# Turning token tiles on VectorE in 32x32 blocks, with x gathered from DRAM in quarter rows

## The chip, the cores and the metric

The kernel runs on one core of a Trainium2 chip. The metric is the device time of one execution in microseconds (us); several executions are summed up by their median. The profile shows one profiled execution of the same program: its span, from the first to the last instruction, is a little shorter than that execution's time, which also holds what lies around it.

## The reference

Two blocks follow each other. The first is a linear attention with decay; its result, the heads laid side by side, is x, with 512 features for each of 4 x 768 = 3,072 tokens. The second is a mixture of 8 experts in which a token can keep the expert of the token before it:

```python
def _moe_ref(x, w_gate, w_local, w1, w2):
    ...
    for b in range(B):
        prev_e = -1
        for s in range(S):
            fresh_e = int(np.argmax(logits[b, s]))
            if s == 0 or local_gate[b, s] < 0.5:
                e = fresh_e
            else:
                e = prev_e if prev_e >= 0 else fresh_e
            prev_e = e
            ...
            h = np.maximum(x[b, s] @ w1[e], 0.0)
            out[b, s] = p[e] * (h @ w2[e])
```

Each token goes through one expert only: 512 features to 1,024 hidden ones, and back to 512. Everything is float32.

## The kernel before, in words

**Attention, 24 steps.** A step takes 128 tokens of one sequence (6 chunks x 4 sequences). It loads 1 MB of q, k and v into one of six buffers `inp` (`loaded`, L156, from the SP queue, five steps ahead), multiplies by decays on GpSimd (`prepare`), and makes scores, the part from the state, and the mix with v on TensorE (`scores`, `from_state`, `mix`). The result `xc` lies with features in the partitions. One step later `rows_of` (L241) turns it with four TensorE transposes into token rows, copies them on ScalarE from PSUM into `xn`, and stores them from ScalarE's DMA queue as 128 rows of `x_dram`, 2 KB each. `xn` has two buffers.

**Routing, between the steps.** After each four steps `gates` and `logits` make the gate logits. The table `extras` (L665) hangs the routing work on fixed steps: which expert each token has, which rank among that expert's tokens, and, inverted, which token sits in each of the 128 slots of an expert tile. `by_slots` (L547) makes this inversion with small matmuls against one-hot masks; from its result it computes `gidx`, the row of `x_dram` for each slot, and `rows_out` (L573) computes `sidx`, the row of the output. This is done twice: for the first five tiles (KA = 5), which only need the tokens of the first 12 steps, during the attention; and for all others while the first expert tiles run (from `brought(1, ...)` on, L768). `span(i)` gives the tiles of each of the two sets.

**Experts.** In this data there are 24 full tiles of 128 slots and 3 half tiles of 64 tokens. For each full tile g:

- `ahead(g)` (L625) calls `collect` (L619): one indirect DMA from GpSimd fetches the 128 rows of the tile into `xgt[g % 2]`, slot by slot in the partitions;
- `turned(g)` (L633) makes four 128x128 transposes on TensorE into a PSUM tile `po1`, and VectorE copies the result to `xtt[g % 2]`, features in the partitions (L637). For tile 0 `first_turned` (L628) does the same in the PSUM tile `pr`;
- `hidden(g, half)` (L639) multiplies by w1: 64 matmul records of 128 columns (each float32 matmul shows as two), ReLU on ScalarE;
- `output(g)` (L650) multiplies by w2 into PSUM: 16 records of 512 columns;
- `written(g)` (L655): VectorE scales by the token's probability into `y`, and GpSimd scatters the rows to the output with an indirect DMA.

`weights(g)` (L608) loads the 2 MB of w1 and the 2 MB of w2 of a tile's expert from the SP queue, when the expert differs from that of the tile two before. Half tiles run beside full ones (`ahead_half`, `turned_half`, `hidden_of_half`, `output_of_half`, L784 to L831). They carry 64 tokens, every one in two partitions, and are turned in four transposes as well.

**What sets the order.** TensorE, VectorE and SP execute in the order in which the program is written (`manual_schedule`); ScalarE's and GpSimd's orders come from a scheduler. [...] In the expert loop, `turned(g + 1)` stands between `hidden(g, 1)` and `output(g)`, and `ahead(g + 2)` ahead of `hidden(g, 0)`. The order at the start of the experts is: the last `mix`, `rows_of(22)`, `first_turned`, `hidden(0, 0)`, `rows_of(23)`, `gates(5)`, `ahead(2)`, `hidden(0, 1)`. Completion of GpSimd's DMAs is signalled on eight semaphores, which the DMAs take in turn; an issue waits until the last one on the same semaphore has landed.

Of the kernel before, what the change touches and what calls it, by code (L numbers as in the profile page):

```python
# [8 lines left out]
F32 = mybir.dt.float32  # L9
# [33 lines left out]
CA = 3  # L43
NA = B * CA
PARTS = [(0, 8), (8, NA), (NA, NT)]
LOADS = 6
QUARTERS = [5, 9, 13, 17]
WARM = 10
# [12 lines left out]
def kernel(  # L61
# [13 lines left out]

    dram = ctx.enter_context(tc.tile_pool(name="dram", bufs=1, space=bass.MemoryType.DRAM))
    x_dram = dram.tile([N, DM], F32, name="x_dram")
    lt = route.tile([P, NT, E + 1], F32, name="lt")  # L80
    moe = ctx.enter_context(tc.tile_pool(name="moe", bufs=2))
    rt = ctx.enter_context(tc.tile_pool(name="rt", bufs=1))
# [158 lines left out]
    def rows_of(s):  # L241
        px = pg.tile([P, DM], F32, name="pk1")
        for a in range(A):
            nc.tensor.transpose(px[:, P * a:P * a + P], xc[:, a, ORDER[s][0]], ident)  # L244
        xn = moe.tile([P, DM], F32, name="xn")
        nc.scalar.copy(xn, px)  # L246
        nc.scalar.dma_start(out=x_dram[P * s:P * s + P, :], in_=xn)

    def gates(k):

# [23 lines left out]
    beforeb = const.tile([P, P], BF16, name="beforeb")  # L274
    dupb = const.tile([P, P], BF16, name="dupb")
    upper = const.tile([P, 1], F32, name="upper")
    ones8 = const.tile([P, E], F32, name="ones8")
    down = const.tile([P, E], F32, name="down")
    go = [const.tile([P, E, hi - lo + 1], BF16, name=f"go{i}") for i, (lo, hi) in enumerate(PARTS)]
# [16 lines left out]
    def constants_2():  # L296
        nc.vector.tensor_copy(count, ints[0][:, :G + 1])
        nc.vector.tensor_copy(whole, ints[0][:, P:P + G + 1])
        nc.vector.tensor_copy(identb, ident)
        nc.vector.tensor_scalar(down, count[:, :E], -1.0, float(E), ALU.mult, ALU.add)  # L300

    def constants_3():
# [6 lines left out]
    def constants_4():  # L309
        for half in range(2):  # L310
            nc.vector.tensor_copy(dupb[:, HP * half:HP * half + HP], ident[:, :HP])
        nc.vector.tensor_reduce(upper, ident[:, HP:], axis=AX.X, op=ALU.add)


    gidx = [route.tile([P, n], U32, name=f"gidx{i}") for i, n in enumerate((KA, G - KA))]
    sidx = [route.tile([P, n], U32, name=f"sidx{i}") for i, n in enumerate((KA, G - KA))]
    gate = [route.tile([P, n], F32, name=f"gate{i}") for i, n in enumerate((KA, G - KA))]
    owner = [route.tile([1, n], I32, name=f"owner{i}") for i, n in enumerate((KA, G - KA))]
# [97 lines left out]
    def chances(i):  # L416

        lo, hi = PARTS[i]
        n = hi - lo
        if i == 2:  # L420
            room = act.tile([P, DM], F32, name="room", bufs=1)
        else:
            room = att.tile([P, DM], F32, name="kd", bufs=3)
        prob = room[:, :n * E].rearrange("p (n e) -> p n e", e=E)
        den, pick = (room[:, k:k + n] for k in (n * E, n * (E + 1)))
        nc.vector.tensor_tensor(prob, lt[:, lo:hi, :E], nows["mx", i].unsqueeze(2).broadcast_to([P, n, E]), ALU.subtract)
        nc.scalar.activation(prob, prob, ACT.Exp)
        nc.vector.tensor_reduce(den, prob, axis=AX.X, op=ALU.add)
        nc.vector.tensor_scalar(den, den, 1e-9, None, ALU.add)
        nc.vector.reciprocal(den, den)  # L430
        nc.vector.tensor_tensor(prob, prob, hot_of(i).rearrange("p e t -> p t e"), ALU.mult)
        nc.vector.tensor_reduce(pick, prob, axis=AX.X, op=ALU.add)
        nc.vector.tensor_tensor(pick, pick, den, ALU.mult)
        for k in range(2, 5):
            nc.vector.tensor_copy(parts[:, lo:hi, k], pick)
            if k < 4:
                nc.vector.tensor_tensor(pick, pick, parts[:, lo:hi, k], ALU.subtract)

    def span(i):
        return ((0, KA), (KA, G))[i]  # L440
# [106 lines left out]
    def by_slots(i, ks):  # L547

        (g0, g1), val = span(i), nows["val"]
        w = g1 - g0  # L550
        pinv = pr[:, 2 * P:2 * P + len(ks) * w]
        cols = [(j, t) for j in range(2 + i) for t in range(PARTS[j][1] - PARTS[j][0])]
        for j, t in cols:
            nc.tensor.matmul(pinv, lhsT=onehots[j][:, t],
                             rhs=val[:, PARTS[j][0] + t].rearrange("p k g -> p (k g)"),
                             start=(j, t) == cols[0], stop=(j, t) == cols[-1], skip_group_check=True)
        got = pools[i].tile([P, len(ks), w], F32, name=f"got{i}_{ks[0]}", bufs=1)
        nc.vector.tensor_copy(got, pinv.rearrange("p (k g) -> p k g", k=len(ks)))
        if 0 in ks:

            src = nows["src"] = pools[i].tile([P, w], F32, name=f"src{i}", bufs=1)
            nc.vector.tensor_scalar(src, got[:, 0], -float(P), 0.0, ALU.add, ALU.max)
            nc.vector.tensor_tensor(gidx[i], src, got[:, 1], ALU.add)
            nows["got"] = got
        if i:
            few = nows["few"] = act.tile([P, len(ks), E], BF16, name="few", bufs=1)
            nc.vector.tensor_copy(few, got[:, :, w - E:])
        if 4 in ks:
            k = ks.index(2)
            nc.vector.tensor_tensor(got[:, k], got[:, k], got[:, k + 1], ALU.add)  # L570
            nc.vector.tensor_tensor(gate[i], got[:, k], got[:, k + 2], ALU.add)

    def rows_out(i):  # L573

        got = nows["got"]
        nc.vector.tensor_scalar(got[:, 0], got[:, 0], 0.0, float(SKIP), ALU.is_equal, ALU.mult)
        nc.vector.tensor_tensor(sidx[i], got[:, 0], gidx[i], ALU.add)

    def both_halves():

# [31 lines left out]
        nc.sync.dma_start(out=w2t[g % 2], in_=w2_src(e), cond=other, cond_hint=False)  # L612


    xgt = [moe.tile([P, DM], F32, name=f"xg{i}", bufs=1) for i in range(2)]
    xtt = [moe.tile([P, DT, P], F32, name=f"xt{i}", bufs=1) for i in range(2)]
    pys = []

    def collect(xg, i, j):  # L619
        n = N if i else NA * P  # L620
        nc.gpsimd.indirect_dma_start(out=xg, out_offset=None, in_=x_dram[:n, :],  # L621
                                     in_offset=bass.IndirectOffsetOnAxis(ap=gidx[i][:, j:j + 1], axis=0),
                                     bounds_check=n - 1, oob_is_err=False)

    def ahead(g):  # L625
        collect(xgt[g % 2], *at(g))

    def first_turned():  # L628
        for d in range(DT):
            nc.tensor.transpose(pr[:, P * d:P * d + P], xgt[0][:, P * d:P * d + P], ident)  # L630
        nc.vector.tensor_copy(xtt[0].rearrange("p d i -> p (d i)"), pr)  # L631

    def turned(g):  # L633
        pt = pg.tile([P, DT, P], F32, name="po1")
        for d in range(DT):
            nc.tensor.transpose(pt[:, d], xgt[g % 2][:, P * d:P * d + P], ident)  # L636
        nc.vector.tensor_copy(xtt[g % 2], pt)  # L637

    def hidden(g, half):  # L639
        if not half:  # L640
# [14 lines left out]
    def written(g):  # L655
# [12 lines left out]
        (12, 0): lambda: ranks(0), (13, 0): lambda: fresh_experts(1), (14, 0): lambda: (along_sequences(1), masks(0)),  # L668
        (15, 0): lambda: experts_of(1), (16, 0): lambda: ranks(1), (17, 0): first_tiles,
        (18, 0): tokens_to_first_tiles, (19, 0): lambda: (brought(0, (0, 1)), masks(1)),  # L670
        (19, 1): lambda: by_slots(0, (0, 1)), (20, 0): lambda: (ahead(0), ahead(1), rows_out(0)),
        (21, 0): lambda: chances(0), (22, 0): lambda: chances(1), (23, 0): lambda: brought(0, (2, 3, 4)),
    }

    def extra_work(s, k):
# [3 lines left out]
    with tc.manual_schedule(engines={PE, DVE, SP}):  # L679
# [17 lines left out]
        for s in range(NS):  # L697
            if s + LOADS - 1 < NS:
                loaded(s + LOADS - 1)
            if s + 3 < NS:  # L700
                prepare(s + 3)
            if s in QUARTERS:
                j = QUARTERS.index(s)
                nc.sync.dma_start(out=w1t[0][:, j], in_=w1_src(0)[:, j])
            if s == NS - 4:
                nc.sync.dma_start(out=w2t[0], in_=w2_src(0))
                nc.sync.dma_start(out=w1t[1], in_=w1_src(1))
                nc.sync.dma_start(out=w2t[1], in_=w2_src(1))
                weights(0)
                weights(1)  # L710
            if s + 1 < NS:
                scores(s + 1)
            if s == 0:
                query_powers()
            from_state(s)
            extra_work(s, 0)
            if s % B == 0 and s:
                gates(s // B - 1)
            mix(s)
            if s:  # L720
                rows_of(s - 1)
            if s + 1 == NS:
                first_turned()
            if s % B == 0 and s:
                logits(s // B - 1)
            extra_work(s, 1)
# [44 lines left out]
        by_slots(1, (0, 1, 2, 3, 4))  # L771
        turned(4)
        finished(3)
        both_halves()
        ahead(5)
        ahead(6)
# [11 lines left out]
        nc.sync.dma_start(out=w2t[2], in_=w2_src(e))  # L788

    def ahead_half(h):  # L790
        xg = act.tile([P, DM], F32, name="xgh")
        collect(xg, 1, GF - KA + h)
        return xg

    def turned_half(xg):
        for d in range(DT):
            nc.tensor.transpose(pr[:, P * d:P * d + P], xg[:, P * d:P * d + P], ident)
        xt = act.tile([P, DT, HP], F32, name="xth")
        nc.vector.tensor_copy(xt, pr.rearrange("p (d i) -> p d i", i=P)[:, :, :HP])
        return xt  # L800

    def hidden_of_half(xt):
# [145 lines left out]
```

## Time and profile before

| | |
|---|---|
| median of 3 runs | 494.95 us (493.7 to 496.34) |
| profiled execution | 494.8 us, span 493.0 us |
| TensorE matmul busy | 475.2 us, 96% of the span |
| VectorE, ScalarE, GpSimd busy | 127.3, 84.7, 106.8 us |
| mean granted TensorE clock | 0.991 |
| DMA | 146.42 MB, mean 297 GB/s |
| indirect gathers of full tiles (L621) | 24, 1,041 ns each on GpSimd; issue to landing 3.4 / 7.0 / 8.0 us (least, median, most) |

How to read it: PE is TensorE's matmul side and PEld its weight load, DVE is VectorE, ACT ScalarE, POOL GpSimd, SP the engine that issues most DMAs. In the page's second part each digit is the busy tenth of a fortieth of the span (12.3 us). In a timeline a row shows start, duration, engine, line, operation, output and input, and in brackets how long the engine had idled and what ended it. Matmul durations overlap (their ends are modelled), so the distance between starts is the safer measure. [...]

### The profile page before, as it was taken

To read this page: it belongs to the slowest core of one execution; us is meant where nothing else is said; L and a number is where in the kernel's file an instruction comes from. 1 tells how busy PE (TensorE), PEld (TensorE's weight loads), DVE (VectorE), ACT (ScalarE), POOL (GpSimd) and SP (SyncE) were. 2 spreads that over 40 slices of the span, in tenths; PEclk is the share of its full clock that TensorE was granted. 3 is DMA by queue.
4 is the path that set the end of the run, shared out by engine and by line. 5 is a ranking of instruction groups with operands and counts; after the bars stand their busy time and mean duration, and the time that the engine had idled before them with its cause. 6 is when DMAs were issued, how large, how long until landed. Compare 5 with 4: busy or idle time off the path is not lost. (4 is left out here: it accounts for less than half of the span.)

```text
span 493.0 us, 10193 instructions
## 1 busy us (share of the span) xinstructions
PE 475.2 (96%) x4231; PEld 351.6 (71%) x4231; DVE 127.3 (26%) x315; ACT 84.7 (17%) x212; POOL 106.8 (22%) x118
## 2 busy tenths in 40 slices
PE   6999999989999999999999999999999999999992
PEld 5877788776777667658657856876667777666770
DVE  6645677652367301011010101101110110110000
ACT  2256656331110000000000001000000000000000
POOL 5575564300101300221011100201101101110000
PEclk9899999999999999999999999999999999999997
DMA  7999999996788999999999997699954980894000
GB/s 272 411 418 380 352 342 330 401 368 233 260 319 292 324 378 399 395 376 397 398 333 386 398 398 277 211 330 319 327 194 157 310 314 31 284 332 169 23 25 17
DMA packets 49850, 146.42 MB, mean 297 GB/s; under 512 B 3244, under 2 KB 3244, under 8 KB 46960
## 3 DMA queue, kind: packets, MB, share of 16 engines
q1 hardware_dynamic: 42096, 125.86, 69.9%
q0 software_dynamic: 4224, 13.37, 7.1%
q10 hardware_dynamic: 3456, 6.29, 3.4%
q8 instruction: 36, 0.59, 0.5%
q14 instruction: 38, 0.31, 0.2%
HBM read 153.90 MB, written 12.98 MB: 338 GB/s over the span
## 5 line engine op out<-in xcount | busy, mean ns | idle before, releaser
L646 PEld LDWEIGHTS ps<-xt,w 128*128 128x128 f32 x1536 | 175.0, 192 | 14.0 <-issue 12.9
L646 PE MATMUL ps<-xt,w 128*128 128x128 f32 x1536 | 177.1, 276 | 0.8 <-DVE xt L631 0.8
L653 PE MATMUL pk<-w,ht 128*128 128x512 f32 x384 | 168.8, 592 | 0.0
L653 PEld LDWEIGHTS pk<-w,ht 128*128 128x128 f32 x384 | 71.1, 190 | 80.4 <-issue 80.4
L648 ACT ACTIVATE ht<-ps 128x512 f32<-128x512 f32 x48 | 28.7, 598 | 314.7 <-PE ps L646 314.2
L659 POOL DMA_INDIRECT out_dram<-y,sidx x24 | 24.6, 1026 | 196.3 <-DVE y L658 179.3
L658 DVE TENSOR_SCALAR y<-pk,gate 128x512 f32<-128x512 f32 x24 | 18.0, 751 | 146.0 <-PE pk L653 140.6
L637 DVE COPY xt<-po 128x512 f32<-128x512 f32 x23 | 15.9, 691 | 143.2 <-PE po L636 143.1
L621 POOL DMA_INDIRECT xg<-x_dram,gidx x24 | 25.0, 1041 | 121.2 <-PE po L636 84.1
L189 DVE TENSOR_TENSOR sm<-ps,mask 128x512 f32<-128x512 f32 x46 | 29.6, 685 | 15.1 <-PE ps L185 15.0
L165 POOL TENSOR_TENSOR qd<-inp,lamq 128x512 f32<-128x512 f32 x20 | 25.6, 1282 | 23.3 <-PE po L212 8.8
L185 PE MATMUL ps<-inp 64*64 64x128 f32 x736 | 26.3, 282 | 2.0 <-DMA inp<-in_qkv_dram 2.0
L225 PE MATMUL po<-sm,inp 128*64 128x128 f32 x384 | 26.9, 284 | 0.3 <-DMA inp<-in_qkv_dram 0.3
L225 PEld LDWEIGHTS po<-sm,inp 128*64 128x64 f32 x384 | 21.1, 140 | 7.5 <-issue 6.6
L168 POOL TENSOR_TENSOR kd<-inp,rev 128x512 f32<-128x512 f32 x20 | 22.4, 1122 | 16.1 <-PE pk L234 7.6
L185 PEld LDWEIGHTS ps<-inp 64*64 64x64 f32 x736 | 20.6, 136 | 5.6 <-issue 4.6
L246 ACT COPY xn<-pk 128x512 f32<-128x512 f32 x24 | 14.1, 588 | 30.6 <-DMA x_dram<-xn 19.8
L216 ACT ACTIVATE kv<-kv,lamq 128x64 f32<-128x64 f32 x64 | 17.1, 337 | 9.8 <-PE po L212 6.4
L228 ACT COPY xc<-po 128x256 f32<-128x256 f32 x48 | 15.3, 371 | 14.2 <-PE po L225 14.0
L244 PE MATMUL pk<-ident,xc 128*128 128x128 f32 x96 | 15.7, 286 | 0.0
L234 PE MATMUL pk<-inp,kd 128*64 128x64 f32 x320 | 13.2, 222 | 1.2 <-issue 1.1
L636 PE MATMUL po<-ident,xg 128*128 128x128 f32 x92 | 13.8, 273 | 0.0
(182 smaller groups left out, 223.6 us busy)
## 6 DMA issues: line engine op xcount, KB each, us to landing
w<-in_w_dram SPq DMA_DIRECT2D x57, 2048.0 KB
inp<-in_qkv_dram SPq DMA_DIRECT2D x22, 1024.0 KB
x_dram<-xn ACTq DMA_DIRECT2D x24, 256.0 KB
inp<-in_qkv_dram SPq DMA_DIRECT2D x4, 512.0 KB
w<-in_w_dram SPq DMA_DIRECT2D x4, 512.0 KB
xg<-x_dram,gidx POOLq DMA_INDIRECT x24, 7.0
out_dram<-y,sidx POOLq DMA_INDIRECT x24, 6.9
xgh<-x_dram,gidx POOLq DMA_INDIRECT x3, 6.4
```

The source lines that it names most:

```text
L165: nc.gpsimd.tensor_tensor(qd, x[:, 0].rearrange("p (a i) -> p a i", i=P), lamq, ALU.mult)
L168: nc.gpsimd.tensor_tensor(kd.rearrange("p (h d) -> p h d", d=DH), x[:, 2].rearrange("p (h d) -> p h d", d=DH), rev.unsqueeze(2).broadcast_ ...
L185: nc.tensor.matmul(ps[u][js, a], lhsT=kt[rows, a, js], rhs=qt[rows, a], start=True, stop=True, skip_group_check=True)
L189: nc.vector.tensor_tensor(sm[:, u], ps[u], mask[:, u], ALU.mult)
L216: nc.scalar.mul(kv[:, a], kv[:, a], lamq[:, a, P - 1:P])
L225: nc.tensor.matmul(head(a, u), lhsT=vn[:, a, u], rhs=sm[:, u, a], start=(not c and a < 2), stop=True, skip_group_check=True)
L621: nc.gpsimd.indirect_dma_start(out=xg, out_offset=None, in_=x_dram[:n, :], in_offset=bass.IndirectOffsetOnAxis(ap=gidx[i][:, j:j + 1], axi ...
L646: nc.tensor.matmul(ph[:, i], lhsT=w1t[g % 2][:, d, P * f:P * f + P], rhs=xtt[g % 2][:, d], start=(d == 0), stop=(d == DT - 1))
L648: nc.scalar.activation(hts[g][:, FT // 2 * half:FT // 2 * half + FT // 2], ph, ACT.Relu)
L653: nc.tensor.matmul(pys[g % 2], lhsT=ht[:, f], rhs=w2t[g % 2][:, f], start=(f == 0), stop=(f == FT - 1))
L658: nc.vector.tensor_scalar(y, pys[g % 2], gate[i][:, j:j + 1], None, ALU.mult)
L659: nc.gpsimd.indirect_dma_start(out=out, out_offset=bass.IndirectOffsetOnAxis(ap=sidx[i][:, j:j + 1], axis=0), in_=y, in_offset=None, bound ...
```

## The change

A tile is turned without TensorE. VectorE's transpose works on blocks of 32x32 [...]. So the data has to arrive with each block already in its group:

- `x_dram` becomes 4 x 3,072 quarter rows of 128 floats (512 B). Quarter q of a token holds those features whose place in each group of 128 lies in the q-th 32. `rows_of` writes `xn` in that order, and its store has four pieces per partition; `xn` gets four buffers.
- A gather becomes four indirect DMAs (two for a half tile). The c-th fetches, for the slots 32c to 32c + 31, quarter q into partition group q.
- `turn` is one VectorE transpose of 128 x 512 (128 x 256 for a half tile) from SBUF to SBUF. The transposes on TensorE, `first_turned`, and the PSUM copies go.
- `gidx` has four indices per slot and partition. A new `wrapped(i)` spreads each slot's row number over the four partition groups with two small matmuls against `same`, and VectorE adds the quarter's number. It stands one step after `by_slots(0)` for the first set (at `(20, 1)`, after the logits of that step), and after `finished(3)` for the second.
- `ahead(0)`, `ahead(1)` and `rows_out(0)` move from step `(20, 0)` to `(21, 0)`, `chances(0)` from `(21, 0)` to `(21, 1)`; `turned(0)` stands at `(23, 1)`, behind `brought(0, (2, 3, 4))`.
- Some constants are added (`block`, `same`, `quarter`), with six VectorE operations in the first steps.

The order that the changed program has on GpSimd differs in one respect besides: scatter 3 now stands ahead of the gathers of tiles 5 and 6, and the gather of tile 7 ahead of scatter 4.

```diff
-    x_dram = dram.tile([N, DM], F32, name="x_dram")
+    x_dram = dram.tile([Q * N, P], F32, name="x_dram")
...
-        xn = moe.tile([P, DM], F32, name="xn")
-        nc.scalar.copy(xn, px)
-        nc.scalar.dma_start(out=x_dram[P * s:P * s + P, :], in_=xn)
+        xn = moe.tile([P, Q, A, QP], F32, name="xn", bufs=4)
+        nc.scalar.copy(xn.rearrange("p q a r -> p a q r"), px.rearrange("p (a q r) -> p a q r", a=A, q=Q))
+        nc.scalar.dma_start(out=x_dram[Q * P * s:Q * P * s + Q * P, :].rearrange("(q p) k -> p q k", q=Q),
+                            in_=xn.rearrange("p q a r -> p q (a r)"))
...
-            nc.vector.tensor_tensor(gidx[i], src, got[:, 1], ALU.add)
+            nc.vector.tensor_copy(src[:, 1], got[:, 1])
+            wrap = nows["wrap"] = pools[i].tile([P, 2, w, Q], BF16, name=f"wrap{i}", bufs=1)
+            nc.vector.tensor_tensor(wrap, src.unsqueeze(3).broadcast_to([P, 2, w, Q]),
+                                    block.unsqueeze(2).broadcast_to([P, 2, w, Q]), ALU.mult)
...
+    def wrapped(i):
+
+        w = span(i)[1] - span(i)[0]
+        pidx = pr[:, :w * Q]
+        for k in range(2):
+            nc.tensor.matmul(pidx, lhsT=same.rearrange("p c q -> p (c q)"),
+                             rhs=nows["wrap"][:, k].rearrange("p g c -> p (g c)"),
+                             start=not k, stop=k == 1, skip_group_check=True)
+        nc.vector.tensor_scalar(gidx[i].rearrange("p g c -> p (g c)"), pidx, quarter, None, ALU.add)
...
     def collect(xg, i, j):
-        n = N if i else NA * P
-        nc.gpsimd.indirect_dma_start(out=xg, out_offset=None, in_=x_dram[:n, :],
-                                     in_offset=bass.IndirectOffsetOnAxis(ap=gidx[i][:, j:j + 1], axis=0),
-                                     bounds_check=n - 1, oob_is_err=False)
+
+        n = Q * (N if i else NA * P)
+        for c in range(xg.shape[1]):
+            nc.gpsimd.indirect_dma_start(out=xg[:, c], out_offset=None, in_=x_dram[:n, :],
+                                         in_offset=bass.IndirectOffsetOnAxis(ap=gidx[i][:, j, c:c + 1], axis=0),
+                                         bounds_check=n - 1, oob_is_err=False)
+
+    def turn(xt, xg):
+        nc.vector.transpose(out=xt.rearrange("p d (c t) -> p c d t", t=QP),
+                            in_=xg.rearrange("p c (d r) -> p c d r", r=QP))
...
     def turned(g):
-        pt = pg.tile([P, DT, P], F32, name="po1")
-        for d in range(DT):
-            nc.tensor.transpose(pt[:, d], xgt[g % 2][:, P * d:P * d + P], ident)
-        nc.vector.tensor_copy(xtt[g % 2], pt)
+        turn(xtt[g % 2], xgt[g % 2])
...
-        (19, 1): lambda: by_slots(0, (0, 1)), (20, 0): lambda: (ahead(0), ahead(1), rows_out(0)),
-        (21, 0): lambda: chances(0), (22, 0): lambda: chances(1), (23, 0): lambda: brought(0, (2, 3, 4)),
+        (19, 1): lambda: by_slots(0, (0, 1)), (20, 1): lambda: wrapped(0),
+        (21, 0): lambda: (ahead(0), ahead(1), rows_out(0)),
+        (21, 1): lambda: chances(0), (22, 0): lambda: chances(1), (23, 0): lambda: brought(0, (2, 3, 4)),
+        (23, 1): lambda: turned(0),
...
-            if s + 1 == NS:
-                first_turned()
...
         finished(3)
+        wrapped(1)
         both_halves()
```

## The prediction

> **What bounds the kernel now.** I read the page's first two parts, then the windows table by stage, then the timeline of TensorE (PE) over the expert tiles.
>
> ```profile
> PE 475.2 (96%) x4231; PEld 351.6 (71%) x4231; DVE 127.3 (26%) x315; ACT 84.7 (17%) x212; POOL 106.8 (22%) x118
> ...
> PE   6999999989999999999999999999999999999992
> ...
> PEclk9899999999999999999999999999999999999997
> DMA  7999999996788999999999997699954980894000
> ```
>
> PE is busy almost everywhere, and DMA as well; the page cannot say which of the two sets the pace. Modelled matmul ends hide gaps, so I go by start times. Two tiles near the end:
>
> ```profile
> 455.54 7.31 PE L646 MATMUL ps<-xt,w 128*128 128x128 f32 x64
> 462.68 0.60 PE L636 MATMUL po<-ident,xg 128*128 128x128 f32 x4
> 463.12 7.03 PE L653 MATMUL pk<-w,ht 128*128 128x512 f32 x16
> 469.99 7.31 PE L646 MATMUL ps<-xt,w 128*128 128x128 f32 x64
> 477.13 7.03 PE L653 MATMUL pk<-w,ht 128*128 128x512 f32 x16
> ```
>
> Between starts: first layer 7.14 us, four transposes 0.44 us, second layer 6.87 us. The last tile has no transposes, and its second layer follows the first after the same 7.14 us (469.99 to 477.13): nothing but the transposes stands between the layers. The period of 14.45 us is held by all tiles from 318 us on, and by those before with their half tiles and routing added; the PE waits list shows 1.6 us in all from 100 to 460 us. So PE sets the pace of the expert stage.
>
> The attention stage (to about 105 us) is closer to a tie:
>
> ```profile
> 12.00:24.00 12.00, 11.05 (x212) 9.71 (x216) 7.37 (x18) 3.11 (x8) 6.84 (x7) 0.86 1.02 409
> 24.00:36.00 12.00, 11.55 (x261) 9.42 (x256) 5.65 (x13) 5.58 (x17) 8.16 (x8) 1.00 1.02 419
> 48.00:60.00 12.00, 12.00 (x268) 9.74 (x266) 8.29 (x21) 7.33 (x25) 7.77 (x7) 1.00 0.96 339
> 60.00:72.00 12.00, 11.40 (x261) 9.96 (x258) 9.35 (x23) 6.24 (x20) 6.83 (x6) 1.00 0.96 341
> ```
>
> The columns after the window are busy time of PE, weight load, DVE, ACT, POOL, then clock, DMA share, GB/s. DMA can move 409 to 419 GB/s, and from 48 us on it is asked for only some 340, because SP waits for PE to free input buffers (64.1 us at L158, 18 times). PE leads here too, with DMA not far behind.
>
> [...] The trace before has no DVE transpose; its PSUM copies of the same size (L637) take 691 ns. [...] its packet records show medians of 84, 159 and 309 ns for 2,048, 4,096 and 8,192 B, which is 9 ns plus 75 ns per 2 KB; no 512 B packet is in it. [...] 0.86 over the 12 us from 12 us on is 12 x 0.14 / 0.5 = 3.4 us at half clock, right after PE had idled from about 11 to 13 us.
>
> **The change, part by part.**
>
> *Transposes off PE.* 23 full tiles (L636, 92 records) and 3 half tiles (L797, 12 records) lose 0.435 us each: 26 x 0.435 = -11.3 us, all on the path. The first tile's set (L630) is counted below. In their place DVE does 24 + 3 block transposes, where it did PSUM copies. I take 0.7 us each; [...] DVE is under 20% busy after 200 us, and `turned(g+1)` can run as soon as the gather has landed and hidden(g-1) has let go of `xt`, a second layer earlier than PE needs it. Queued behind it on DVE is y(g), which comes later anyway. Without that cover each would cost its 0.7 us.
>
> *Four gathers for one.* POOL gets 72 more full-tile gathers and 3 more half-tile ones (two for one). Their spacing is in the trace:
>
> ```profile
> 91.89 1.21 POOL L621 DMA_INDIRECT xg<-x_dram,gidx  x1 [2.28 <-DVE gidx L563]
> 93.41 1.01 POOL L621 DMA_INDIRECT xg<-x_dram,gidx  x1 [0.30 <-issue]
> ...
> 105.50 0.60 PE L630 MATMUL pr<-ident,xg 128*128 128x128 f32 x4
> 106.88 3.84 PE L646 MATMUL ps<-xt,w 128*128 128x128 f32 x32 [0.78 <-DVE xt L631]
> ```
>
> 1.52 us for the first and 1.35 us for later pairs (164.39 to 165.74). A tile then costs POOL 4 x 1.35 + 1.35 for its scatter = 6.8 us of 14. In the steady state that is free: a gather is issued over 20 us before its use. The built program shows eight completion semaphores for POOL's DMAs, taken in turn; with five DMAs a tile each waits for the one eight back, over a tile old, which landed (about 7 us) long ago. At the two places where the index has just been made, it is not free:
>
> *First tile.* The index now also needs `wrapped(0)`: two small matmuls behind the logits transposes of step 20 (they start at 95.49 us and end about 96.1), then one DVE operation: about 96.9 instead of 91.6. POOL begins at 97.1; the fourth gather is issued at 97.1 + 1.52 + 2 x 1.35 = 101.3.
>
> ```profile
> xg<-x_dram,gidx POOLq DMA_INDIRECT x3, 7.9
> ...
> q10 hardware_dynamic: 3456, 6.29, 3.4%
> ```
>
> The first line is the median from issue to landing between 85 and 110 us. With 6.4 (it carries a quarter of the bytes; estimate) to 7.9 us the rows are there at 107.7 to 109.2, plus 0.7 for the transpose. The tile's matmuls start at about 109.4 instead of 106.88: +2.5 us (0 to +5). PE comes free at 105.50, so it idles some 4 us, above what cost it the clock at 12 us; one spell of 3.4 us at half clock costs 1.7 us (0 to 2.5). Tile 1's gathers are issued by 107 and land by 115, before 127.
>
> *Tile 5.* `wrapped(1)` stands behind output(3), where the index was ready 7 us earlier. Counted from the end of output(3): y(3) and its scatter hold POOL to +2.5, the fourth gather goes at +6.6, lands at +13 to +13.6, is turned at +14.3. PE has hidden(4) and output(4) until then, 14.1 us and a little. I take +0.3 (0 to +2). The four index matmuls add 0.3 us.
>
> *The x rows.* 24 stores of 256 KB become 512 B pieces: 12,288 packets for 3,072. By the fit above a 512 B packet takes 9 + 19 = 28 ns. Before: 3,072 x 85 / 16 engines = 16.3 us (the q10 line gives the same: 3.4% of 493). After: 12,288 x 28 / 16 = 21.5, so +5.2 us of DMA time. The seven windows of 12 us from 12 to 96 us moved 31.5 MB, 76 us at 414 GB/s, and so had 8 us to spare. Zero on the path; it cannot be a gain, since the bytes are the same and the packets more. Above 28 ns I know no bound but the rival below. The gathers, at +27 ns for each 2 KB, add 0.2 us of DMA time a tile: nothing, since weights between 170 and 310 us ask for about 370 of 400 GB/s. PE gaining 3% asks for 380.
>
> *The rest.* `xn` goes to four buffers and takes away ACT's 19.8 us of waiting for stores; little of it reaches PE (0 to -1). Nine DVE operations of about 0.2 us are added in the attention stage (0 to +1). Together 0.
>
> Sum: -11.3 + 2.5 + 1.7 + 0.3 + 0.3 = -6.5. The profiled execution took 494.8 us (span 493.0), as good as the median of 494.95: 488.4 us.
>
> **Rivals.**
> *Quick start:* gathers land in the 3.4 us that is the fastest seen[...]: -11.3 + 0.6 = 484 us. Against it: DMA is full from 85 to 115 us.
> *Late start:* the eight gathers go slower through the full queues, or the first tile meets two clock spells: +6 and +2.5, tile 5 +2, so -0.2 or so: 494.5 us, no change. For it: every delay here adds up on one idle PE. Against it: 8.0 us is the longest landing in the whole trace.
> *Slower, by one mechanism:* the 512 B stores saturate the DMA engines in the attention stage. The slack is 8 us before 96 us plus some 12 us until the last prefetched weights are needed (132 us; DMA falls quiet at about 120). Extra time over 20 us decides, which is (20 + 16.3) x 16 / 12,288 = 47 ns per packet. At 64 ns the extra is 33 us, 13 beyond the slack: 488.4 + 13 = 501 us. [...] Against it: three sizes lie on one line, and its intercept is 9 ns.
>
> **How the numbers follow.** Forecast 488.4 (485.5 to 491.5): 0.60. Quick start: 0.12. Late start: 0.16. Saturated stores: 0.12. Faster by over 0.5% (below 492.5; about what a measurement can tell from no change): 0.60 + 0.12, less 0.02 for the forecast's edge = 0.70. Within: 0.18, the late start and that edge. Slower: 0.12. The range 484 to 496 leaves out the last case and little else.
>
> **What would show it.** Right: the four records of L636 are gone, and the tile period is 14.0 us; POOL shows four gathers 1.35 us apart; the first matmuls of the experts start near 109.4 us, with a dip of the clock in that slice; x stores take 28 ns a packet. Wrong: a tile period that stays at 14.4 (PE waits for weights, or for DVE); L185 waiting for `inp`, which is the saturated store; a first tile beyond 112 us.

## The result, and the profile after

The changed kernel took 515.48 us (median of 4 runs, 512.22 to 517.3), the kernel before 495.64 beside it (4 runs, 493.7 to 496.91): a ratio of 1.040, 95% interval 1.033 to 1.047. It was slower, where 488.4 us was forecast. The same program, unaltered, took 483.5, 483.5 and 484.4 us in three later measurements (ratios 0.979, 0.976 and 0.976), and 511.8 us in a fourth (two executions, 507.9 and 515.7); what differs between them is the subject of what follows.

The profiled execution took 516.9 us, span 515.1, mean TensorE clock 0.972. The page of the changed kernel:

```profile
PE 477.3 (93%) x4127; PEld 346.1 (67%) x4127; DVE 129.2 (25%) x327; ACT 86.2 (17%) x212; POOL 181.3 (35%) x193
...
PE   6999997969999983999899999999999999979995
...
PEclk9999999969999996999799999999999999999999
```

TensorE (PE) has lost the transposes (4,127 records for 4,231), and yet is busy 2 us longer. There are new or deeper holes at the 7th, 9th, 16th and 36th slice, and dips of the clock in the 9th, 16th and 20th. POOL's busy time went from 106.8 to 181.3 us. The period of a tile is as forecast where nothing disturbs it; the timeline of PE, changed kernel:

```profile
364.10 7.31 PE L673 MATMUL ps<-xt,w 128*128 128x128 f32 x64
...
378.11 1.05 PE L673 MATMUL ps<-xt,w 128*128 128x128 f32 x8
```

364.10 to 378.11 is 14.01 us. So the loss is not in the period. PE's list of waits has two kinds on top that were not there before, both with no releaser that the profile knows (it writes `issue` or `remote` for that):

```profile
PE pk L680 <- issue: 11.7, 3, 10.2
PE ps L188 <- issue: 4.6, 10, 0.7
```

The longest, 10.2 us, stands in the second layer of tile 4. The timelines of POOL, PE, ACT and DVE there (start, duration, what; in brackets the idle time before it and its releaser):

```profile
181.63 0.98 POOL L686 DMA_INDIRECT out_dram<-y,sidx  x1 [14.25 <-DVE gidx L599]
...
199.87 0.99 POOL L652 DMA_INDIRECT xg<-x_dram,gidx  x1 [0.30 <-issue]
```

```profile
180.53 7.39 PE L673 MATMUL ps<-xt,w 128*128 128x128 f32 x64
187.76 3.60 PE L680 MATMUL pk<-w,ht 128*128 128x512 f32 x8
201.61 2.93 PE L680 MATMUL pk<-w,ht 128*128 128x512 f32 x3 [10.25 <-issue]
```

```profile
185.31 0.60 ACT L675 ACTIVATE ht<-ps 128x512 f32<-128x512 f32 x1 [12.63 <-PE ps L673]
200.96 0.60 ACT L675 ACTIVATE ht<-ps 128x512 f32<-128x512 f32 x1 [15.05 <-remote]
```

```profile
192.93 0.71 DVE L657 STREAM_TRANSPOSE xt<-xg 128x512 f32<-128x512 f32 x1 [9.52 <-DMA xg<-x_dram,gidx]
```

Read them together. POOL issues 15 indirect DMAs in one unbroken run, 1.30 us apart, from 181.63 to 200.86: scatter 3, the gathers of tiles 5 and 6 and of the half tile, and those of tile 7. PE ends the 64 matmuls of `hidden(4)` at 187.92 and goes on with the half of `output(4)` that it can do. The second ReLU (ACT, L675) needs nothing but those matmuls, and starts 13 us later, at 200.96. DVE's next transpose waits for the same signal, to have `xt` back, and starts at 200.96 too; the next weight load on SP was issued at 200.95. The transpose in the fence, which waits for a DMA, ran in the middle, at 192.93. So rows and index were there; what was missing is TensorE's signal. The trace marks the last of those matmuls as one that updates a semaphore, and the ReLU, the transpose at 200.96 and the load at 200.95 as waiting for that semaphore; such an update is called an increment here, and a signal is held when its increment comes late. The trace's record of this semaphore has it: 187.92 the matmul's end, 200.93 the increment.

The same happened at the first tile (PE's timeline):

```profile
103.31 0.65 PE L188 MATMUL ps<-inp 64*64 64x128 f32 x4
...
119.33 3.74 PE L673 MATMUL ps<-xt,w 128*128 128x128 f32 x32
```

Eight gathers run from 100.67 to 110.99. PE's last scores, 1.1 us of work elsewhere, trickle until 113.0; the first expert matmuls start at 119.33, where 109.4 was forecast.

Set against a later measurement of the same program (483.24 us, span 481.5; first label below), the starts of the tiles tell where the 33.6 us between the two spans lie:

| stretch | its run of indirect DMAs on POOL | lost against the later trace |
|---|---|---|
| to the first expert matmul | 8, at 100.67 | +11.0 us, 3.3 of it ahead of the run |
| tiles 0 to 3 | 4 at most | -0.1 |
| tile 4 | 15, at 181.63 | +12.9 |
| tiles 5 and 6 | the run of 13 begins in tile 6, at 230.59 | -1.1 |
| tile 7 | its end, at 247.28 | +6.4 |
| tiles 8 to 19 | 5 at most | 0.0 |
| tile 20 | 12, at 445.08 | +4.4 |
| to the end | single scatters | 0.0 |

Some 30 us of it lie in four places, at the four runs of eight and more. The other 3.3 us were lost in the attention steps, before any indirect DMA (the first gather starts at 100.67 against 97.36); in the other slow measurement of this program it starts at 96.59, so they are not part of what follows. Some 13 us of the loss are the clock (an estimate: the clock missing from the means of 0.972 and 0.998, times the spans): the trace has it at 0.5 from 107.52 to 117.76, from 196.27 to 206.51 and from 247.47 to 254.30 us, at the first three of the four places. The rest is idling.

### The profile page after: what moved, and what is told of

Same layout as the page of the kernel before. It is cut to its first block, busy times and chain, and to the rows that moved or that the text cites. A ratio compares the mean times of both kernels' runs of the same rounds, so it can differ in the third digit from the quotient of the medians.

```text
span 515.1 us, 10152 instructions
## 1 busy us (share of the span) xinstructions
PE 477.3 (93%) x4127; PEld 346.1 (67%) x4127; DVE 129.2 (25%) x327; ACT 86.2 (17%) x212; POOL 181.3 (35%) x193
## 5 line engine op out<-in xcount | busy, mean ns | idle before, releaser
L673 PEld LDWEIGHTS ps<-xt,w 128*128 128x128 f32 x1536 | 178.1, 194 | 17.7 <-issue 17.6
L673 PE MATMUL ps<-xt,w 128*128 128x128 f32 x1536 | 181.6, 278 | 3.8 <-issue 3.5
L680 PE MATMUL pk<-w,ht 128*128 128x512 f32 x384 | 172.3, 601 | 11.8 <-issue 11.7
L652 POOL DMA_INDIRECT xg<-x_dram,gidx x96 | 96.6, 1006 | 71.6 <-issue 25.3
L675 ACT ACTIVATE ht<-ps 128x512 f32<-128x512 f32 x48 | 28.7, 597 | 330.1 <-PE ps L673 283.1
L188 PE MATMUL ps<-inp 64*64 64x128 f32 x736 | 30.7, 280 | 7.7 <-issue 4.6
L188 PEld LDWEIGHTS ps<-inp 64*64 64x64 f32 x736 | 21.7, 134 | 14.6 <-issue 12.4
L657 DVE STREAM_TRANSPOSE xt<-xg 128x512 f32<-128x512 f32 x24 | 16.9, 704 | 22.6 <-DMA xg<-x_dram,gidx 11.9
L215 PE MATMUL po<-qd,kv 64*64 64x128 f32 x320 | 14.5, 287 | 1.1 <-ACT xc L231 1.0
```

The source lines that it names most:

```text
L188: nc.tensor.matmul(ps[u][js, a], lhsT=kt[rows, a, js], rhs=qt[rows, a], start=True, stop=True, skip_group_check=True)
L652: nc.gpsimd.indirect_dma_start(out=xg[:, c], out_offset=None, in_=x_dram[:n, :], in_offset=bass.IndirectOffsetOnAxis(ap=gidx[i][:, j, c:c ...
L673: nc.tensor.matmul(ph[:, i], lhsT=w1t[g % 2][:, d, P * f:P * f + P], rhs=xtt[g % 2][:, d], start=(d == 0), stop=(d == DT - 1))
L675: nc.scalar.activation(hts[g][:, FT // 2 * half:FT // 2 * half + FT // 2], ph, ACT.Relu)
L680: nc.tensor.matmul(pys[g % 2], lhsT=ht[:, f], rhs=w2t[g % 2][:, f], start=(f == 0), stop=(f == FT - 1))
```

## The experiments

Three theories were on record. Theory 1, held signals: while GpSimd issues indirect DMAs in a long unbroken run, TensorE's semaphore increments arrive late, and whoever waits for them stands still. Theory 2: the new index and the gathers are simply late. Theory 3: the stores of x in 512 B pieces fill the DMA engines.

**Stores alone, and added gathers in the kernel before.**

```diff
 stores:
+        xn = moe.tile([P, Q, A, QP], F32, name="xn", bufs=4)
+        nc.scalar.copy(xn.rearrange("p q a r -> p a q r"), px.rearrange("p (a q r) -> p a q r", a=A, q=Q))
+        nc.scalar.dma_start(out=x_dram[Q * P * s:Q * P * s + Q * P, :].rearrange("(q p) k -> p q k", q=Q), ...)
-        nc.gpsimd.indirect_dma_start(out=xg, out_offset=None, in_=x_dram[:n, :],
+        nc.gpsimd.indirect_dma_start(out=xg, out_offset=None, in_=x_dram.rearrange("(n q) k -> n (q k)", q=Q)[:n, :],
...
 dose, dose_tiny, dose_paused:
+    def burst(g):
+        n, every, pause = DOSES.get(g, (0, 0, 0))
+        for c in range(n):
+            nc.gpsimd.indirect_dma_start(out=spare_rows[:, c], ...)
+            if every and c % every == every - 1:
+                for _ in range(pause):
+                    nc.gpsimd.memset(rest, 0.0)
```

> The kernel before with the changed copy and store of x alone: quarter rows of 512 B in DRAM, four buffers for xn. The gathers read 2 KB rows of this layout, so that they fetch rows of other tokens (the rows' contents are not those of the reference). Theory 1: the stores have no part in the loss, 495.6 with -1 to +2. Theory 3: they bear most of the 20 us by which the changed kernel is slower, 505 us or more, seen as TensorE waiting for inp before 100 us.

> The kernel before, with gathers of 512 B rows that nobody uses added behind the scatters of tiles 14, 16 and 18: 3, 6 and 10, which makes unbroken runs of 5, 8 and 11 indirect DMAs on GpSimd (also: GpSimd's order is written out from tile 5 on). Theory 1 (held signals: in a long unbroken run of GpSimd's indirect DMAs TensorE's semaphore increments reach nobody until the run ends): the run of 5 costs nothing, that of 8 some 1 to 4 us, that of 11 (14.3 us long) 3 to 9 us[...]; 495.6 + 4 to 13 = 500 to 508 us. Theory 2 (the changed kernel is only late because its indices and rows come late): nobody waits for these rows, so 495.6 within 1 us. Theory 3 (the stores in 512 B pieces fill the DMA engines): no such store here, 495.6 within 1 us.

> As the run with 3, 6 and 10 added gathers, but each gathers rows of 64 B, an eighth of the bytes [...]. Theory 1[...]: the same loss as with 512 B rows within 1.5 us. If the bytes on their way or the time of landing do it: under a third of that loss. Theories 2 and 3: 495.6 within 1 us.

> The kernel before with 10 unused gathers of 512 B rows behind each of the scatters of tiles 14, 16 and 18, but broken up by memsets of 0.52 us on GpSimd: one after each gather, two after each gather, and four after each fourth gather. Theory 1: no gather follows another without a pause, so in the first two places nothing is held: TensorE loses under 0.5 us in each, and in the third (runs of 5, 4 and 2) under 1 us; 495 to 497 us with 30 added gathers, less than with the 19 unbroken ones. If the number of gathers within some 15 us counted and not the unbroken run: over 3 us lost in each place, 505 us or more. Theories 2 and 3: 495.6 within 1 us.

`stores` took 495.46 us, ratio 1.0016 (0.9994 to 1.0038); of its 15 executions 13 lie within 493.5 to 497.6 us, and two, at 617.7 and 2,760.8 us, have no trace that could explain them. Theory 3 falls.

`dose` took 515.66 us (1.043), `dose_tiny` 511.88 (1.035), `dose_paused` 529.78 (1.072). The totals of the first two look like theory 1, and that of the one with pauses like its refutation; both readings are wrong. The run of ten added gathers in `dose`, and PE beside it:

```profile
429.04 1.02 POOL L673 DMA_INDIRECT out_dram<-y,sidx  x1 [12.09 <-DVE y L672]
...
446.02 1.03 POOL L635 DMA_INDIRECT xg<-x_dram,gidx  x1 [0.31 <-PE ps L660]
```

```profile
427.80 7.31 PE L660 MATMUL ps<-xt,w 128*128 128x128 f32 x64
...
442.25 7.31 PE L660 MATMUL ps<-xt,w 128*128 128x128 f32 x64
451.41 0.63 PE L650 MATMUL po<-ident,xg 128*128 128x128 f32 x4 [1.85 <-DMA xg<-x_dram,gidx]
```

A run of 14 from 429.04 to 447.05, and PE keeps its period of 14.45 us through it; no increment of PE was over 0.15 us late anywhere in these four traces. The only loss here is 1.85 us for a gather that had to queue behind the added ones. Most of the rest came from the written order that I needed to place the gathers: it put half tiles' gathers behind a scatter and a full tile's gather, and PE waited 7.1 and 3.6 us for `xgh`, each with a clock spell (a stretch at half the clock, 6.8 and 3.4 us long) behind it; the second layers there take 8.69 and 8.73 us for 7.03. So these three tell nothing for theory 1 by their times, and by their traces they contradict its first form: a long run alone is not enough. (No changed kernel ran beside them. That this was a quiet measurement, one in which no signal is held, is taken from `dose`'s pair of gathers at 93.59: at such a pair the kernel before can show late increments, as told further below.)

**The changed kernel again, its order, and its pauses.**

```diff
 ordered:
-    with tc.manual_schedule(engines={PE, DVE, SP}):
+    with tc.manual_schedule(engines={PE, DVE, SP, mybir.EngineType.Pool}):
...
 spread, besides (two memsets in place of three in spread2):
+            if c == 3 or (c == 1 and (i, j) != (0, 0)):
+                for _ in range(3):
+                    nc.gpsimd.memset(rest, 0.0)
 four_in_before:
+        for _ in range(3):
+            turns[0] += 1
+            nc.gpsimd.indirect_dma_start(out=spare_rows[:, turns[0] % 8], ...)
```

> The changed kernel once more, unaltered, as the mark for the three others of this call. All theories: 515 us, 1.04 of the kernel before. Were it near 490, the 20 us would belong to the place where it ran and not to the kernel.

> The changed kernel with GpSimd's order written out in program order: scatters ahead of later gathers, the first half tile's gathers behind those of tile 6, the gather of tile 7 behind scatter 4. That breaks up the runs of indirect DMAs at 182, 231 and 445 us in part; the run of 8 for tiles 0 and 1 stays. Theory 1 (in a long unbroken run of indirect DMAs TensorE's signals are held): the first stall of 9 to 10 us stays, of the later 20 us between a third and two thirds go: 500 to 508 us. Theory 2 (indices and rows come late): 515 with -2 to +2.

> As the run with the written order, and on GpSimd a pause of three memsets (about 1.9 us) after each second gather, for tile 0 after the fourth alone; no run of indirect DMAs is longer than 4. Theory 1: no stall is left, tile period 14.0 us, first expert matmuls near 110 us: 486 to 491 us. Theory 2: gathers come later than in the changed kernel, so 515 or more.

> The kernel before with three gathers of 512 B rows that nobody uses behind each gather, the number that the changed kernel issues; the index, the transposes on TensorE and the stores are those of before. The scheduler puts 12 of the added gathers in one run at about 100 us and others later. The unused gathers at 370 to 447 us held nothing, in runs of 8 and 14. Theory 1 as first stated would still have it: signals held at 100 to 116 us, 505 us or more. If it is something else in the changed kernel (its wait on four semaphores per tile, its index, VectorE's transposes): no signal held, and only rows that come late behind the added gathers: 495 to 503 us.

The changed kernel took 483.49 us (0.979, 0.976 to 0.982), `ordered` 485.1, `spread` 492.54, `four_in_before` 503.34. I had not expected the first. Its POOL order is the same as in the first measurement, with the same runs; at tile 4:

```profile
170.70 0.98 POOL L686 DMA_INDIRECT out_dram<-y,sidx  x1 [14.25 <-DVE gidx L599]
...
188.97 1.00 POOL L652 DMA_INDIRECT xg<-x_dram,gidx  x1 [0.31 <-issue]
```

```profile
169.61 7.39 PE L673 MATMUL ps<-xt,w 128*128 128x128 f32 x64
```

```profile
177.03 0.60 ACT L675 ACTIVATE ht<-ps 128x512 f32<-128x512 f32 x1 [2.92 <-PE ps L673]
```

The second ReLU starts 0.03 us after the matmuls' end, not 13. So the program alone does not bring the holding about; where it occurs, the runs are the places where it is seen, the long ones above all. `ordered` still has runs of 8 and 15, so the written order alone does not break up the longest one. In such a quiet measurement pauses only cost: in `spread` PE waited 6.1 us for rows of half tiles. In `four_in_before` it waited 5.5 us for weights, and no signal was held, in runs of up to 35.

**The third and fourth measurement of it, shorter pauses, and the transposes back on TensorE.** In `spread2` the half tile's gathers also go ahead of the full tile's. In `pe_turns` each tile gets the four transposes and a PSUM copy back:

```diff
     def turned(g):
-        turn(xtt[g % 2], xgt[g % 2])
+        pt = pg.tile([P, DT, P], F32, name="po1") if g else pr.rearrange("p (d i) -> p d i", d=DT)
+        for d in range(DT):
+            nc.tensor.transpose(pt[:, d], xgt[g % 2][:, d], ident)
+        nc.vector.tensor_copy(xtt[g % 2], pt)
...
```

> The changed kernel unaltered, a third time; it took 515 us in the first measurement, with TensorE's signals held up in long runs of GpSimd's indirect DMAs, and 483.5 us in the second, with the same runs of DMAs and no signal held. Theory 1a (the holding belongs to the place, a chip, and the runs of indirect DMAs only call it up there): either near 483 to 485 with no signal held, or near 512 to 517 with signals held behind runs of more than five; nothing between. Theory 1b (it comes and goes at random from one execution to the next): times spread between 483 and 515 within this one measurement.

> The changed kernel with GpSimd's order written out, the half tile's gathers ahead of the full tile's, and a pause of two memsets (1.3 us) after each second gather (for tile 0 after the fourth). Longest run of indirect DMAs: 4 to 5. If the place holds signals: theory 1 expects no loss from it here, 484 to 490 us where the changed kernel takes 515. If it does not: 484 to 488, up to 4 us behind the changed kernel for gathers that come later.

> The changed kernel unaltered, a fourth time, to see how often the 515 us of the first measurement come back. Theory 1a (a matter of the place): 483 to 485 us with no signal held, or 512 to 517 with signals held in runs of more than five indirect DMAs. Theory 1b (at random from one execution to the next): times between these two.

> The changed kernel with its tiles turned by TensorE after all: four 128x128 transposes and a PSUM copy per tile, as before the change, with the four gathers, the index and the stores of after. (The transposed blocks are not put in their places, so the features reach the experts in the wrong order.) Without held signals: the 23 full and 3 half tiles get back their 0.435 us on TensorE, 11.3 us, and 0.4 for the first: 483.5 + 11.7 = 495 us, the time of the kernel before. If the gain came from anything else than the transposes (xn's four buffers, the earlier gathers): nearer to 484. With held signals (theory 1): they stay, since the runs of indirect DMAs do: 520 us or more.

483.45 us (0.976), 482.48 (0.975), 484.36 (0.976) and 503.07 us (1.011). No signal was held in any of the four. `pe_turns` is 18.7 us slower than the changed kernel beside it, 7 more than I had expected for the transposes. Its timeline shows why; PE at tile 5:

```profile
182.69 0.30 PE L666 MATMUL po<-ident,xg 128*128 128x128 f32 x1 [1.69 <-DMA xg<-x_dram,gidx]
...
185.77 0.47 PE L666 MATMUL po<-ident,xg 128*128 128x128 f32 x1 [0.81 <-DMA xg<-x_dram,gidx]
```

A transpose on PE stands ahead of `output(4)` and takes PE's turn while it waits for the four gathers: 3.7 us here, and a clock spell of 6.8 us at half speed behind it (3.4 lost; `output(4)` takes 9.65 us for 7.03). With the turn on VectorE PE did not stand still there: in the second measurement `output(4)` starts at 176.83 and `hidden(5)` at 183.70, without a gap. With 11.7 for the transposes that is 18.8 us, the difference.

**Meeting it again.** I moved the first index and its gathers one half step ahead (the expectations say two), once with the long runs and once with the pauses of `spread2`:

```diff
-        (19, 1): lambda: by_slots(0, (0, 1)), (20, 1): lambda: wrapped(0),
-        (21, 0): lambda: (ahead(0), ahead(1), rows_out(0)),
+        (19, 1): lambda: by_slots(0, (0, 1)), (20, 0): lambda: wrapped(0),
+        (20, 1): lambda: (ahead(0), ahead(1)), (21, 0): lambda: rows_out(0),
```

> The changed kernel with its first index two half steps earlier: wrapped(0) at (20, 0), ahead of the gates of that step, and the gathers of tiles 0 and 1 at (20, 1). Its runs of indirect DMAs on GpSimd are those of the changed kernel. Where no signal is held: the first gather leaves at about 95 us instead of 97.4, the rows are turned before TensorE comes free, and the wait of 1.8 us ahead of the first expert matmuls goes: 484 - 1.8 = 482 us. Where signals are held as in the first measurement: 510 us or more, and theory 1a (a matter of the place) has a second case.

> The early index together with the pauses on GpSimd after each second gather and the half tile's gathers ahead of the full tile's. Where no signal is held: 480 to 482 us, as fast as the early index alone or a little faster. Where signals are held: theory 1 expects no run long enough to matter, 480 to 487 us; were it over 500 us there, the length of the runs would not be what decides.

506.2 us (1.023, 1.016 to 1.029) and, measured beside it on the same chip, 484.56 us (0.977, 0.971 to 0.982). On that chip the changed kernel had taken 484.36 shortly before, so the chip alone does not decide. In `early` the signals were held again. ACT's second ReLU at tile 4 in `early`, whose run of 15 goes from 176.91 to 196.21; PE ended its matmuls at 183.21:

```profile
191.20 0.60 ACT L675 ACTIVATE ht<-ps 128x512 f32<-128x512 f32 x1 [10.07 <-remote]
```

and POOL and ACT at the same place in `early_spread`, where the second ReLU comes on time (matmuls' end 180.38):

```profile
180.40 1.00 POOL L653 DMA_INDIRECT xg<-x_dram,gidx  x1 [0.30 <-issue]
181.40 1.12 POOL L658 MEMSET rest<- 128x512 f32 x2
```

```profile
180.42 0.60 ACT L679 ACTIVATE ht<-ps 128x512 f32<-128x512 f32 x1 [2.11 <-PE ps L677]
```

That `early_spread` ran under the same circumstances shows in its one run of four, tile 0's gathers from 95.97 to 101.07. DVE waits there for scores that PE had ended at 98.57:

```profile
101.77 1.29 DVE L192 TENSOR_TENSOR sm<-ps,mask 128x512 f32<-128x512 f32 x2 [3.82 <-remote]
```

So the pauses bounded the holding and did not end it: those increments came 3.2 us late, 0.7 us past the run's end. The last steps of the attention (from the mix of step 20 to that of step 23) take 13.97 us, where `spread2` and `after_fourth` take 10.47, and the first expert matmuls start at 111.69, where `spread2` has 107.13:

```profile
111.69 3.50 PE L677 MATMUL ps<-xt,w 128*128 128x128 f32 x29 [0.61 <-DVE xt L661]
```

From there on the two kernels lie within half a us of this distance; their spans differ by 4.3 us.

> The changed kernel with the early index once more; it took 506 us with held signals, in a call where the same kernel with pauses took 484.6. If the holding belongs to the circumstances of a measurement and not to this kernel: 482 us (the 484 of the changed kernel less its first wait of 1.8 us) if this call is a quiet one, and then the changed kernel beside it takes 484; or 505 to 515 for both. If the early gathers themselves call it up: 505 us for this one and 484 for the changed kernel.

> The changed kernel unaltered, beside the early index on the same chip: in the same state as it, 484 us if no signal is held, 505 to 517 us if signals are.

510.0 us (1.029, 1.020 to 1.037) and 511.79 us (2 runs): both slow, on another chip. The unaltered kernel repeats the trace of the first measurement: holes at the same four runs, and the second ReLU of tile 4 late by 11 us. The early gathers do not call the holding up, since the kernel without them shows it too, and they gain little here: the first expert matmuls start at 114.0 and 114.7.

> The changed kernel with the order written out and the pauses of 1.3 us on GpSimd, which took 482.5 us where no signal was held. Theory 1: with runs of at most five indirect DMAs it takes 482 to 488 us in a measurement with held signals as well, 25 us less than the changed kernel has there. If only the early index made the version with pauses fast in the one such measurement so far, this one is over 500 us.

> The kernel before with three unused gathers behind each gather, in runs of up to 12; 503.3 us and no signal held the first time. If signals are held in this measurement, and the runs of indirect DMAs alone call it up, without VectorE's transposes, the quarter rows' index or their stores: signals of TensorE late by several us in its runs of 12, and a time above the 503, 508 us or more. If they are held only with the changed kernel's other parts: 503 again. In a quiet measurement: 503, and nothing is told.

483.7 us (0.978, 0.971 to 0.986) and 500.96 (1.013). No signal was held even in the added gathers' run of 35. `spread2_again` has the same run of four for tile 0 in which `early_spread` had increments up to 4.2 us late, and there none was over 0.15 us late; so this was a quiet measurement, and the two tell nothing on the cure.

The second ReLU's signal at tile 4 sums it up:

| measurement of | matmuls end | increment | time |
|---|---|---|---|
| changed kernel, first | 187.92 | 200.93 | 515.5 us |
| changed kernel, fifth | 183.26 | 194.19 | 511.8 |
| `early` / `early_again` | 183.21 / 182.68 | 191.17 / 194.29 | 506.2 / 510.0 |
| changed kernel, second to fourth | 177.00 / 175.98 / 177.59 | 177.01 / 175.99 / 177.60 | 483.5 / 483.5 / 484.4 |
| `early_spread`, beside `early` | 180.38 | 180.40 | 484.6 |

## Why the prediction was wrong, step by step

*Transposes off PE, -11.3 us.* Right: the period is 14.01 us. A transpose on VectorE takes 0.70 us where I took 0.7. `pe_turns` bears the price out, and adds what I had not counted: a turn on PE also waits for its rows in PE's turn.

*Four gathers for one.* This is the step that failed: an overlap that was taken to be free. Its numbers hold: 1.30 us from one to the next (I said 1.35), eight semaphores, no wait on them that matters. What failed is "In the steady state that is free": I asked who waits for POOL's gathers, and not what a long run of them does to others. I had read that the built order puts the gather of tile 7 ahead of scatter 4, and did not count the run of 15 that this makes. Under circumstances that are not known such a run delays TensorE's signals by up to 13 us, and in the first measurement the four runs cost about 30 of the 33.6 us.

*First tile, +2.5 and a clock spell of 1.7.* In a quiet measurement: 108.30 for 109.4 forecast, PE idle 1.75 us for about 4, no clock spell. The term was too large by 2.8 us: 1.1 because the fourth gather (issued at 101.47, turned from 107.53 on) needed at most 6.1 us to land, and 1.7 for the clock spell. That is the outcome of the rival "quick start", which gave 484 and had no term for the clock, though not its reason, a landing within 3.4 us. The clock spell was an estimate from a single case: the gap that I pointed to was 1.97 us long (10.98 to 12.95), and the clock stands at 0.5 from 12.83 to 16.24. Here 1.75 us brought no spell, nor did 1.85 us in `dose`; how long PE has to stand still for one is not shown. In the first measurement the start is 119.33, past the 112 us that I had named as the sign of being wrong; 3.3 us of this are older than the gathers.

*Tile 5, +0.3.* In a quiet measurement zero: `hidden(5)` follows `output(4)` without a gap (176.83 to 183.70).

*The x rows, 0 on the path.* Right. A 512 B packet took a mean of 27.2 ns where the fit said 28; the page's line is below, and `stores` shows 1.0016 for this part alone. The rival of saturated stores falls.

```profile
q10 hardware_dynamic: 12672, 6.29, 4.1%
```

*The sum.* Without held signals the change gives 483.5 to 484.4 us, at the lower end of the range of 484 to 496 or just below it. With them it gives 505 to 517, beyond its upper end, and no rival of mine had that mechanism. I gave a slower outcome 0.12, all of it to the stores, an estimate that nothing in the trace of before backed. (The terms of the rival "late start" add up to -0.5 and not -0.2, which changes nothing.)

*Could the profile of before have told?* Faintly. Its pair of gathers runs from 91.89 to 94.42. PE ends the gate logits at 93.45 (first line), and ACT, which copies them, starts 1.4 us later, after the run's end; in `dose`, a quiet measurement, 0.06 us lie between the two. The record of TensorE's semaphore says why: four sets of matmuls ended between 92.45 and 94.47, and their increments stand at 94.73 to 95.01, where `dose` has them within 0.05 us.

```profile
92.39 1.06 PE L252 MATMUL pl<-xc,wgt 128*32 128x512 f32 x8
...
94.85 0.59 ACT L255 COPY lg<-pl 128x512 f32<-128x512 f32 x1 [2.31 <-PE po L225]
```

That kernel has neither VectorE's transposes nor quarter rows, so held signals need neither; it has no run over three, and lost next to nothing. But in the same trace, in the run of three at 207.44 to 211.12, no increment was over 0.1 us late.

*What stays open.* What puts a measurement into this condition: it held for all runs of a measurement, in three of eight, and one chip was met with it and without it. Whether long runs cost the kernel before as much: the trials with added gathers fell into quiet measurements. What in a run delays the increments, and why not all of them. Whether pauses or the changed order of POOL did the curing in `early_spread`: they were tried together. The cure itself rests on one pair. Every execution on record has a span and a clock from the profiler, so that its recording plays a part is not excluded.

## What to carry to other kernels

A step moved to an idle queue is not shown to be free by the queue's own waits: count the longest unbroken run of indirect DMAs in the built order, not just the queue's share of a tile, and break it up where there is time. `spread2` was as fast as the changed kernel in quiet measurements (482.5 and 483.7 us for 483.5 and 484.4), and `early_spread`, which shares its pauses and its order, was 21.6 us faster than `early` where signals were held. When an engine stands still with no releaser, look at who resumes at the same instant and what they have in common: here all that stood still waited for one engine's signal, and what waited for DMAs ran. And measure a surprising result a second time before explaining it: the first explanation of the 20 us, that long runs hold signals, left out that most measurements hold none.

## What the runs showed of the hardware that I had not expected

- At tile 4, where signals were held, TensorE's increment came 8.0 (`early`) to 13.0 us (first measurement) after the matmul it stands for, while GpSimd issued indirect DMAs 1.30 us apart. With runs of five in the first measurement there were delays of 0.9 to 2.1 us, up to 1.2 us past the run's end, which cost nothing; with runs of 8 to 15 PE lost 2.4 to 13 us at each. Length alone does not tell the cost: the run of four in `early_spread`, in the attention, cost 3.5 us.
- It need not last to the end of the run, nor begin with it: in `early` the signal came at 191.17, 5 us before the end. In the first measurement's run of 13, from 230.59 on, increments for matmuls that ended at 231.77, 232.66 and 236.53 were on time within 0.02 us, and those due from 239.97 on came from 249.33 on.
- PE itself went slowly in one such run: in the first measurement its last scores took 9.7 us for 1.1 (103.31 to 113.01). At tile 4 it did not: its eight matmuls of the second layer took 3.60 us, half of the 7.03 for 16.
- A block transpose on VectorE took 702 ns (median of 24) for 128 x 512 and 402 (of three) for 128 x 256 float32; a line through these two, an estimate, gives 300 ns for 256 columns and about 100 fixed.
- A memset of 128 x 512 on GpSimd took 0.52 us (522 ns in the kernel before), and two between gathers made a gap of 1.3 us (181.40 to 182.71 in `early_spread`).
